# Splitting a real Fourier transform over the model dimension a second time by parity: four matrices of half the rows and half the columns in place of two

## Chip, core and metric

One core of one Trainium2 chip runs the kernel. The metric is the device time of one execution in microseconds (us); lower is better. Three runs of the kernel before took 1491.76, 1490.05 and 1491.19 us, median 1491.19 us.

## What is computed

```python
x = A_x                                    # (1, 2048, 576), float32
xn = _layernorm(x, axis=-1)
X = jnp.fft.rfft2(xn, axes=(-2, -1))       # over the 2048 rows (s) and the 576 columns (d)
X = X * (w_r + 1j * w_i)                   # weights (2048, 289)
y = jnp.fft.irfft2(X, s=(2048, 576), axes=(-2, -1))
g = x @ w_gate; u = x @ w_up               # (576, 4608) each
return x + y + (_sigmoid(g) * u) @ w_down  # w_down (4608, 576)
```

## The kernel before

Two computations share the core: a gated MLP, and a spectral filter (a two-dimensional real Fourier transform, a product with complex weights, and the inverse).

**The MLP sets the pace.** The 2048 rows are worked in two passes of 1024, and each pass runs 36 units, one for each 128 of the 4608 hidden columns (`unit`, L522). A unit has seven products of seven 512-column matmuls each (L541, tiles pA, pB, pE in PSUM). After every second unit, eight `down` steps (L586) of twelve 288-column matmuls (L597, tile po) add to the output accumulators on VectorE (L602).

**The filter is interleaved.** Between a unit's products stands a call of `beside`, which moves each active generator on by one step, up to its next `yield`. All work of the filter lies in the second pass. Its three stages begin at fixed steps (`U1, U2, U3`, L37), so that one of their tiles starts every 4.5 to 4.8 steps. Below they are called stages U1, U2 and U3:

- U1, `phase1b` (L335, 16 tiles of 128 rows): normalise a tile (L345), fold it about column 288 into an even and an odd half of 289 columns (`eo`, L348), transpose it on TensorE (tile pf, L357), and multiply by two 289x290 matrices, cosine and sine (tile pd, L372). Then the first part of the transform over the rows (tile pa, L383).
- U2, `phase2` (L388, 16 tiles): the second part over the rows (pb, L411), the product with the complex weights on VectorE (z and t2, L418 to L420), and the first part of the inverse (pc, L427).
- U3, `phase3` (L432, 16 tiles): the rest of the inverse over the rows (py, L453), transpose (pz, L465), the inverse over d with two 289x290 matrices (pe, L482), and VectorE adds of the result onto the accumulators (L486 to L489).

**Precision.** The matmuls take operands of type fp32r. `split` (L175) makes of a value a high part (a ScalarE copy into an fp32r tile, L176) and a low part (a VectorE subtraction, L177). A product is the sum of high x high, low x high and high x low. The 289 rows of a transform are two blocks of 128 and a remainder of 33. The remainder's high part, low part and high part again are stacked into one operand of 99 rows (`rp`, fr and z3r), so that one matmul does for it. A transform has thus 2 x (2 x 3 + 1) = 14 matmuls of 290 columns. The stationary operand of each is a 128-column tile of the transposed data (fh, fl, fr in U1; z3h, z3l, z3r in U3), the moving one a row block of the constant matrix (cf, or dit).

**What sets the order.** The tile framework schedules each engine's instructions when the program is built, with waits between engines; on the chip each engine then takes its own in that order. The PSUM tiles pf, pd, pa, pb, pc, py, pz, pe and po all come from one pool of two buffers (`pair`, L141). Most tiles of a stage have one buffer.

In the tables of the page, PE is TensorE, PEld its loading of stationary operands, DVE is VectorE, ACT is ScalarE, POOL is GpSimd, and SPq the queue that issues DMAs.

Of the kernel before, what the change touches and what calls it, by code (L numbers as in the profile page):

```python
# [24 lines left out]
FR = HD + 1 - 2 * P  # L25
# [14 lines left out]
KOF = np.array(list(range(1, 257)) + [0] + list(range(257, 289)))  # L40
# [19 lines left out]
def _constants():  # L60
    out = {}

    d = np.arange(HD + 1)[:, None]
    ang = 2 * np.pi * ((d * KOF[None, :]) % D) / D
    t = np.zeros((P, 2, 5, NQ), np.float32)
    for e, v in ((0, np.cos(ang)), (1, -np.sin(ang))):
        m = np.zeros((HD + 1, NQ))
        m[:, :KD] = v
        if e == 0:
            m[HD] *= 0.5  # L70
        else:
            m[0] = m[HD] = 0.0
            m[:, 256] = m[:, 288] = 0.0
        hi, lo = _split(m)
        for part, w in ((0, hi), (1, lo)):
            t[:, e, 2 * part] = w[:P]
            t[:, e, 2 * part + 1] = w[P:2 * P]
        t[:3 * FR, e, 4] = np.concatenate([hi[2 * P:], hi[2 * P:], lo[2 * P:]])
    out["cf"] = t.reshape(P, 10 * NQ)
# [27 lines left out]
    dd = np.arange(HD + 1)
    ang = 2 * np.pi * ((KOF[:, None] * dd[None, :]) % D) / D
    a = np.where((KOF == 0) | (KOF == HD), 1.0, 2.0)[:, None] / (D * S)
    co = np.zeros((KD, NQ))  # L110
    si = np.zeros((KD, NQ))
    co[:, :HD + 1] = a * np.cos(ang)
    si[:, 1:HD] = (a * np.sin(ang))[:, 1:HD]
    si[256] = 0.0
    si[288] = 0.0
    t = np.zeros((P, 2, 5, NQ), np.float32)
    for e, m in ((0, co), (1, si)):
        hi, lo = _split(m)
        for part, w in ((0, hi), (1, lo)):
            t[:, e, 2 * part] = w[:P]  # L120
            t[:, e, 2 * part + 1] = w[P:2 * P]
        t[:3 * FR, e, 4] = np.concatenate([hi[2 * P:], hi[2 * P:], lo[2 * P:]])
    out["di"] = t.reshape(P, 10 * NQ)
    out["id"] = np.eye(P, dtype=np.float32)
    return out
# [3 lines left out]
def spectral_glu_kernel(ctx: ExitStack, tc: tile.TileContext, x, w_r, w_i, w_gate, w_up, w_down, out):  # L129
# [45 lines left out]
    def split(hi, lo, src, eng=None):  # L175
        nc.scalar.activation(hi, src, AF.Copy)  # L176
        (eng or nc.vector).tensor_tensor(lo, src, f32(hi), op=OP.subtract)  # L177
# [157 lines left out]
    def phase1b(t):  # L335
# [16 lines left out]
        nc.scalar.activation(rp[:, :, 2, :], rem, AF.Copy)  # L352
        yield
        pt = pair(f"pf{t}")
        for e in range(2):
            for k in range(2):
                nc.tensor.transpose(pt[:, 0, (2 * e + k) * P:(2 * e + k + 1) * P], eo[:, e, k * P:(k + 1) * P], idf)  # L357
            nc.tensor.transpose(pt[:3 * FR, 1, e * P:(e + 1) * P].bitcast(F32R), rp[:, e].rearrange("p a b -> p (a b)"), idr)
# [4 lines left out]
        nc.scalar.activation(fr[:3 * FR], pt[:3 * FR, 1, :2 * P].rearrange("p (e s) -> p e s", e=2), AF.Copy)  # L363
        yield
        pd = pair(f"pd{t}")
        for e in range(2):
            steps = []
            for k in range(2):
                steps += [(fh[:, e, k, :], cf[:, e, k, :]), (fl[:, e, k, :], cf[:, e, k, :]), (fh[:, e, k, :], cf[:, e, 2 + k, :])]
            steps.append((fr[:3 * FR, e, :], cf[:3 * FR, e, 4, :]))  # L370
            for n, (l, r) in enumerate(steps):
                nc.tensor.matmul(pd[:, e, :NQ], l, r, start=n == 0, stop=n == len(steps) - 1)  # L372
# [15 lines left out]
    def phase2(i):  # L388
# [25 lines left out]
        nc.scalar.activation(sw[N1:], pb[:N1, :, :KD], AF.Copy)
        z = pool.tile([P, 2, KD], F32, tag="z", name=f"z{i}")
        t2 = pool.tile([P, 2, KD], F32, tag="t2", name=f"t2{i}")
        for q, k in ((slice(0, 256), slice(1, 257)), (slice(256, 257), slice(0, 1)), (slice(257, KD), slice(257, KD))):
            nc.vector.tensor_tensor(z[:, :, q], wr[:, :, k], pb[:, :, q], op=OP.mult)  # L418
# [13 lines left out]
    def phase3(t):  # L432
# [33 lines left out]
        v = pz[:3 * FR, 1, :256].rearrange("p (c a s) -> p c a s", c=2, a=2)
        for sl in range(2):
            nc.tensor.transpose(v[:, :, sl, :].bitcast(F32R), rp[:, sl].rearrange("p a b -> p (a b)"), idr)
# [4 lines left out]
        nc.scalar.activation(zr[:3 * FR], pz[:3 * FR, 1, :256].rearrange("p (c s) -> p c s", c=2), AF.Copy)  # L473
# [2 lines left out]
        for e in range(2):
            steps = []
            for k in range(2):
                steps += [(zh[:, k, e, :], di[:, e, k, :]), (zl[:, k, e, :], di[:, e, k, :]), (zh[:, k, e, :], di[:, e, 2 + k, :])]
            steps.append((zr[:3 * FR, e, :], di[:3 * FR, e, 4, :]))  # L480
            for n, (l, r) in enumerate(steps):
                nc.tensor.matmul(pe[:, e, :NQ], l, r, start=n == 0, stop=n == len(steps) - 1)  # L482
        od = pool.tile([P, HD + 1], F32, tag="od", name=f"od{t}")
        nc.scalar.activation(od, pe[:, 1, :HD + 1], AF.Copy)
# [9 lines left out]
    def stage1():  # L494
        pool = room("1")
        R["cf"] = cf = pool.tile([P, 2, 5, NQ], F32R, name="cf")
        load_r(cf, con["cf"].rearrange("p (e k n) -> p e k n", e=2, k=5))
        yield

    def stage2():  # L500
        pool = room("2")
# [2 lines left out]
        zh = pool.tile([P, 2, NQ], F32R, name="zh")
        zl = pool.tile([P, 2, NQ], F32R, name="zl")
        for z in (zh, zl):
            nc.vector.memset(f32(z)[:, :, KD:], 0.0)
        R["zz"] = [(zh, zl)]
# [247 lines left out]
```

## Time and profile before

| | |
|---|---|
| median of three runs | 1491.19 us (1490.05 to 1491.76) |
| the profiled execution | 1492.63 us, of which 1490.8 us span |
| mean granted TensorE clock | 0.993 |
| PE busy, PEld busy | 1449.1 us (97%), 1277.1 us (86%) |
| DVE, ACT, POOL busy | 963.6 us (65%), 579.5 us (39%), 23.0 us (2%) |
| matmuls of L541 (MLP, first step), L597 (second step) | 3577, 3456 |
| matmuls of pd (L372), of pe (L482) | 224, 224 |

The span runs from the first instruction to the last. A row of the timeline gives the start in us, the time in us, the engine, the line, the operation with output and inputs, the shape, and how many instructions are merged in the row; in brackets stands how long the engine was idle before it and what released it. A matmul's time in such a row is from its issue to the modelled end of its pipeline, and neighbours overlap in it. How fast they follow on each other is read from the starts. A row of the windows gives, for one stretch of the span, each engine's busy time with the count of instructions, then the granted clock, the DMA share and GB/s.

### The profile page before, as it was taken

The page shows a single profiled execution, that of the slowest core. Times are in us where ns is not written, and L with a number is a line of the kernel's source. Part 1 is how long each engine was busy: PE and PEld are TensorE (multiplying, and loading weights), DVE is VectorE, ACT ScalarE, POOL GpSimd, SP SyncE. Part 2 cuts the span into 40 slices and gives each one's busy share as a digit, 9 for nine tenths or more (in the row PEclk, how much of TensorE's full clock was granted, in tenths as well). Part 3 has the DMA queues.
Part 4 walks back from the last instruction along what each step waited for, and adds up shares of the span by engine and source line. Part 5 has one row for each costly group of instructions (what it writes and reads, how often), then busy time and mean ns, then how long its engine had stood idle before and what let it go on. Part 6 is the DMA issues. An engine that isn't in the chain of part 4 may idle for free.

```text
span 1490.8 us, 21461 instructions
## 1 busy us (share of the span) xinstructions
PE 1449.1 (97%) x8229; PEld 1277.1 (86%) x8229; DVE 963.6 (65%) x1628; ACT 579.5 (39%) x965; POOL 23.0 (2%) x44
## 2 busy tenths in 40 slices
PE   3899999999999999999999999999999999999998
PEld 3688888888888888887888888888888899898897
DVE  7989977777777777777465555455566554554543
ACT  3534444333344443334343434343444333333321
POOL 1100000000000000011000000000000000000000
PEclk9899999999999999999999999999999999999999
DMA  6388666666665666665964645487777566753522
GB/s 200 136 280 269 233 219 229 242 239 229 229 216 213 222 231 239 226 212 215 287 215 157 199 160 195 153 258 226 226 251 233 213 234 201 232 166 136 186 94 64
DMA packets 152630, 311.79 MB, mean 209 GB/s; under 512 B 14160, under 2 KB 79952, under 8 KB 147664
## 3 DMA queue, kind: packets, MB, share of 16 engines
q1 hardware_dynamic: 152528, 310.42, 61.7%
q8 instruction: 65, 1.06, 0.3%
q14 instruction: 37, 0.30, 0.1%
HBM read 189.98 MB, written 120.39 MB: 208 GB/s over the span
## 4 chain that ended last, share of the span: by engine, by line
PE 90%; DVE 4%; SPq 2%; ACT 1%; DMA 1%; issue 1%; DVEq 0%; ACTq 0%
PE po L597 29%; PE pB L541 22%; PE pE L541 14%; PE pA L541 14%; PE pd L372 2%; PE pe L482 2%; PE px L322 1%; PE pa L383 1%; PE pc L427 1%; PE pb L411 1%; SPq L257 1%; PE py L453 1%; DMA xt<-in_A_x 0%; DVE xs L284 0%; PE pf L357 0%
## 5 line engine op out<-in xcount | busy, mean ns | idle before, releaser
L597 PE MATMUL po<-wd,hh 128*128 128x288 f32 x2304 | 402.4, 296 | 2.3 <-ACT hh L582 1.7
L541 PE MATMUL pB<-X,w 128*128 128x512 f32 (+1 forms) x1533 | 391.8, 390 | 2.4 <-ACT v L555 1.3
L602 DVE TENSOR_TENSOR acc<-acc,po 128x576 f32<-128x576 f32 x288 | 216.2, 753 | 235.3 <-PE po L597 231.7
L597 PEld LDWEIGHTS po<-wd,hh 128*128 128x128 f32 x2304 | 344.6, 189 | 16.2 <-DVE acc L602 2.5
L541 PEld LDWEIGHTS pB<-X,w 128*128 128x128 f32 x1533 | 278.3, 188 | 55.9 <-ACT v L555 2.7
L541 PE MATMUL pA<-X,w 128*128 128x512 f32 (+1 forms) x1022 | 264.2, 392 | 1.6 <-ACT X L325 0.9
L541 PE MATMUL pE<-X,w 128*128 128x512 f32 (+1 forms) x1022 | 263.5, 393 | 0.7 <-ACT X L325 0.7
L597 PE MATMUL po<-wd,hl 128*128 128x288 f32 x1152 | 246.9, 295 | 0.0
L541 PEld LDWEIGHTS pA<-X,w 128*128 128x128 f32 x1022 | 189.6, 190 | 38.0 <-ACT X L325 1.4
L541 PEld LDWEIGHTS pE<-X,w 128*128 128x128 f32 x1022 | 187.0, 191 | 34.4 <-ACT X L325 1.0
L597 PEld LDWEIGHTS po<-wd,hl 128*128 128x128 f32 x1152 | 186.7, 189 | 0.2 <-DVE hl L583 0.2
L565 ACT ACTIVATE g<-pB 128x512 f32<-128x512 f32 (+1 forms) x73 | 43.3, 593 | 217.2 <-PE pB L541 216.8
L583 DVE TENSOR_TENSOR hl<-y,hh 128x1024 fp32r<-128x1024 f32 x72 | 87.9, 1222 | 25.1 <-ACT hh L582 25.1
L204 ACT ACTIVATE w<-raw 128x1152 fp32r<-128x1152 f32 x36 | 42.1, 1168 | 137.0 <-PE pE L541 115.3
L580 DVE TENSOR_TENSOR y<-y,g 128x1024 f32<-128x1024 f32 x72 | 88.2, 1224 | 5.6
L582 ACT ACTIVATE hh<-y 128x1024 fp32r<-128x1024 f32 x72 | 75.5, 1048 | 10.9 <-DVE y L580 10.5
L569 DVE TENSOR_TENSOR y<-v,pE 128x512 f32<-128x512 f32 (+1 forms) x73 | 49.6, 679 | 45.1 <-PE pE L541 44.9
L562 DVE TENSOR_TENSOR y<-v,pE 128x512 f32<-128x512 f32 (+1 forms) x73 | 49.4, 676 | 38.4 <-ACT v L561 38.1
L548 ACT ACTIVATE pB<-pA 128x512 f32<-128x512 f32 (+1 forms) x73 | 41.9, 574 | 74.0 <-PE pA L541 74.0
L561 ACT ACTIVATE v<-pB 128x512 f32<-128x512 f32 (+1 forms) x73 | 43.2, 592 | 51.0 <-PE pB L541 50.7
L558 ACT ACTIVATE g<-pA 128x512 f32<-128x512 f32 (+1 forms) x73 | 43.1, 591 | 49.3 <-PE pA L541 49.3
L204 ACT ACTIVATE w<-tt 128x768 fp32r<-128x768 f32 x72 | 59.7, 829 | 1.9 <-DVE tt L220 1.9
(123 smaller groups left out, 1303.8 us busy)
## 6 DMA issues: line engine op xcount, KB each, us to landing
wsp<-w SPq DMA_DIRECT2D x36, 2240.0 KB
w<-wsp SPq DMA_DIRECT2D x252, 320.0 KB
wdsp<-wd SPq DMA_DIRECT2D x36, 576.0 KB
wd<-wdsp SPq DMA_DIRECT2D x36, 576.0 KB
std<-in_B_w_down SPq DMA_DIRECT2D x36, 288.0 KB
raw<-in_B_w_gate SPq DMA_DIRECT2D x72, 128.0 KB
raw<-in_B_w_up SPq DMA_DIRECT2D x72, 128.0 KB
sc<-x SPq DMA_DIRECT2D x16, 290.0 KB
```

The lines of the kernel that those rows point to most:

```text
L204: nc.scalar.activation(o[:, :, :3, :], src, AF.Copy)
L541: nc.tensor.matmul(bank[b], w[:, WB[kb], sw, :], X[:, XA[ka], sx, cols], start=b not in seen and j == 0, stop=j == len(STEPS) - 1, skip_gr ...
L558: nc.scalar.activation(g[:, 0], bank["A"], AF.Sigmoid)
L561: nc.scalar.activation(v[:, 1], bank["B"], AF.Copy)
L562: nc.vector.tensor_tensor(y[:, 1], v[:, 1], bank["E"], op=OP.add)
L565: nc.scalar.activation(g[:, 1], bank["B"], AF.Sigmoid)
L569: add = lambda: nc.vector.tensor_tensor(y[:, 0], v[:, 0], bank["E"], op=OP.add)
L580: nc.vector.tensor_tensor(Y, Y, G_, op=OP.mult)
L582: ends.extend([first, lambda: nc.scalar.activation(hh, Y, AF.Copy), lambda: nc.vector.tensor_tensor(hl, Y, f32(hh), op=OP.subtract)])
L583: lambda: nc.vector.tensor_tensor(hl, Y, f32(hh), op=OP.subtract)])
L597: nc.tensor.matmul(pd[:, b, :HD], l[:, c, cols], w[:, k, b * HD:(b + 1) * HD], start=g == 0 and l is hh and k == 0, stop=g == G - 1 and l ...
L602: nc.vector.tensor_tensor(a, a, pd[:, :, :HD], op=OP.add)
```

## The change

The folded halves of U1 are folded once more, about column 144: the even part of the cosine half goes with the even frequencies, its odd part with the odd ones, and the other way round for the sine half. Each of the four combinations is a transform with 145 rows (one block of 128 and a remainder of 17) and 146 or 144 columns. The spectrum's columns are stored in the order of the even frequencies, a zero column, then the odd ones (KOF). The remainders of both parities are stacked into one operand of 6 x 17 = 102 rows, used with two matrices that have zeros in the other parity's rows. The inverse in U3 is split in the same way, and its four results are joined again on VectorE.

In numbers, for each tile: pd and pe are 4 x 4 = 16 matmuls of 146 or 144 columns (14 of 290 before); the transposes stay six. In U1 VectorE has two more operations (f4) and one more small subtraction, ScalarE two more small copies (four of 34 columns in place of two of 66) and a copy of one column. In U2 the product with the weights is done in two column groups in place of three, and reads every second column of the weights. In U3 VectorE has four more operations (cs, 145 or 144 columns), and its four adds onto the accumulators read cs. The constants cf and dit have 12 x 146 = 1752 columns in place of 2900.

```diff
+QD = D // 4 + 1
+HQ = NQ // 2
+QR = QD - 128
-FR = HD + 1 - 2 * P
-KOF = np.array(list(range(1, 257)) + [0] + list(range(257, 289)))
+KOF = np.array(list(range(0, KD, 2)) + [-1] + list(range(1, KD, 2)))
...
-        rp = pool.tile([P, 2, 3, FR], F32R, tag="rp", name=f"rp{t}")
-        rem = eo[:, :, 2 * P:2 * P + FR]
-        split(rp[:, :, 0, :], rp[:, :, 1, :], rem)
-        nc.scalar.activation(rp[:, :, 2, :], rem, AF.Copy)
+        nc.scalar.activation(eo[:, 0, HD:HD + 1], xb[:, HD:HD + 1], AF.Copy)
+        f4 = pool.tile([P, 2, 2, HQ + 1], F32, tag="f4", name=f"f4{t}")
+        for i, op in ((0, OP.add), (1, OP.subtract)):
+            nc.vector.tensor_tensor(f4[:, i, :, :QD], eo[:, :, :QD], eo[:, :, QD - 1:HD + 1][:, :, ::-1], op=op)
+        rp = pool.tile([P, 2, 3, 2, QR], F32R, tag="rp", name=f"rp{t}")
+        for c, rem in ((0, f4[:, :, 0, P:QD]), (1, f4[:, ::-1, 1, P:QD])):
+            split(rp[:, c, 0], rp[:, c, 1], rem)
+            nc.scalar.activation(rp[:, c, 2], rem, AF.Copy)
...
-        for e in range(2):
-            steps = []
-            for k in range(2):
-                steps += [(fh[:, e, k, :], cf[:, e, k, :]), (fl[:, e, k, :], cf[:, e, k, :]), (fh[:, e, k, :], cf[:, e, 2 + k, :])]
-            steps.append((fr[:3 * FR, e, :], cf[:3 * FR, e, 4, :]))
-            for n, (l, r) in enumerate(steps):
-                nc.tensor.matmul(pd[:, e, :NQ], l, r, start=n == 0, stop=n == len(steps) - 1)
+        for c in range(2):
+            for par, q in ((0, slice(0, HQ + 1)), (1, slice(HQ + 1, NQ))):
+                n = q.stop - q.start
+                w = cf[:, c, par, :, :n]
+                steps = ((fh[:, c, par], w[:, 0]), (fl[:, c, par], w[:, 0]), (fh[:, c, par], w[:, 1]), (fr[:6 * QR, c], w[:6 * QR, 2]))
+                for i, (l, r) in enumerate(steps):
+                    nc.tensor.matmul(pd[:, c, q], l, r, start=i == 0, stop=i == len(steps) - 1)
...
-        for q, k in ((slice(0, 256), slice(1, 257)), (slice(256, 257), slice(0, 1)), (slice(257, KD), slice(257, KD))):
+        for q, k in ((slice(0, HQ), slice(0, KD, 2)), (slice(HQ + 1, NQ), slice(1, KD, 2))):
             nc.vector.tensor_tensor(z[:, :, q], wr[:, :, k], pb[:, :, q], op=OP.mult)
             nc.vector.tensor_tensor(t2[:, :, q], wi[:, :, k], sw[:, :, q], op=OP.mult)
...
+        for b in range(2):
+            for c in range(2):
+                par = b ^ c
+                w = di[:, c, par]
+                steps = ((zh[:, par, c], w[:, 0]), (zl[:, par, c], w[:, 0]), (zh[:, par, c], w[:, 1]), (zr[:6 * QR, c], w[:6 * QR, 2]))
+                for i, (l, r) in enumerate(steps):
+                    nc.tensor.matmul(pe[:, b, c * (HQ + 1):(c + 1) * (HQ + 1)], l, r, start=i == 0, stop=i == len(steps) - 1)
...
-        nc.vector.tensor_tensor(lo, lo, od, op=OP.subtract)
-        nc.vector.tensor_tensor(lo, lo, pe[:, 0, :HD + 1], op=OP.add)
+        for c, lo_op, up_op in ((0, OP.add, OP.subtract), (1, OP.subtract, OP.add)):
+            nc.vector.tensor_tensor(cs[:, c, :QD], p0[:, c, :QD], od[:, c, :QD], op=lo_op)
+            nc.vector.tensor_tensor(cs[:, c, QD:][:, ::-1], p0[:, c, :QD - 1], od[:, c, :QD - 1], op=up_op)
+        co, si = cs[:, 0], cs[:, 1]
+        nc.vector.tensor_tensor(lo, lo, co, op=OP.add)
+        nc.vector.tensor_tensor(lo, lo, si, op=OP.subtract)
```

The change moves instructions on every engine. On TensorE, this is the 15th tile of U1 before, from the last transpose into pf to the first products of pd; pE is a product of the MLP, fh, fl and fr are the high part, the low part and the remainder of the transposed tile:

```order
L358 MATMUL pf_8654<-idr,rp_8613 99x128
L541 MATMUL pE_0_8474<-X,w_8273 128x512 x7
L372 MATMUL pd_8681<-cf,fh_8661 128x290
L372 MATMUL pd_8681<-cf,fl_8662 128x290
L372 MATMUL pd_8681<-cf,fh_8661 128x290 x2
L372 MATMUL pd_8681<-cf,fl_8662 128x290
L372 MATMUL pd_8681<-cf,fh_8661 128x290
L372 MATMUL pd_8681<-cf,fr_8663 128x290
```

And the same place now (f is the twice folded tile):

```order
L369 MATMUL pf_8787<-idr,rp_8743 102x128
L557 MATMUL pE_0_8598<-X,w_8381 128x512 x7
L383 MATMUL pd_8814<-cf,fh_8794 128x146
L383 MATMUL pd_8814<-cf,fl_8795 128x146
L383 MATMUL pd_8814<-cf,fh_8794 128x146
L383 MATMUL pd_8814<-cf,fr_8796 128x146
L383 MATMUL pd_8814<-cf,fh_8794 128x144
```

The first product with the remainder fr stood five places behind the first one with fl; it stands two places behind it.

ScalarE at the same tile before, from the copy that makes fh to the copy that makes fr (rp is the remainder of the next tile):

```order
L176 ACTIVATE fh_8661<-pf_8654 128x512
L176 ACTIVATE rp_8752<-eo_8749 128x2x33
L352 ACTIVATE rp_8752<-eo_8749 128x2x33
L363 ACTIVATE fr_8663<-pf_8654 99x256
L176 ACTIVATE ah_8696<-pd_8681 64x290
```

And now:

```order
L182 ACTIVATE fh_8794<-pf_8787 128x512
L182 ACTIVATE rp_8891<-f_8888 128x34
L363 ACTIVATE rp_8891<-f_8888 128x34
L182 ACTIVATE rp_8891<-f_8888 128x34
L363 ACTIVATE rp_8891<-f_8888 128x34
L374 ACTIVATE fr_8796<-pf_8787 102x256
```

Two more copies of the next tile's remainder stand ahead of fr.

TensorE at the second tile of U3 before, from the first product of pe:

```order
L482 MATMUL pe_11462<-dit,z3h_11427 128x290
L541 MATMUL pE_0_11446<-X,w_11230 128x512 x4
L482 MATMUL pe_11462<-dit,z3l_11428 128x290
L482 MATMUL pe_11462<-dit,z3h_11427 128x290 x2
L482 MATMUL pe_11462<-dit,z3l_11428 128x290
L482 MATMUL pe_11462<-dit,z3h_11427 128x290
L541 MATMUL pE_0_11446<-X,w_11230 128x512
L482 MATMUL pe_11462<-dit,z3r_11429 128x290
```

And now:

```order
L493 MATMUL pe_11551<-dit,z3h_11516 128x146
L557 MATMUL pE_0_11535<-X,w_11312 128x512 x3
L493 MATMUL pe_11551<-dit,z3l_11517 128x146
L493 MATMUL pe_11551<-dit,z3h_11516 128x146
L557 MATMUL pE_0_11535<-X,w_11312 128x512 x2
L493 MATMUL pe_11551<-dit,z3r_11518 128x146
```

Between z3l and z3r stood four products of pe and one of the MLP; there stand one of pe and two of the MLP.

More of the change, by code (lines that the diff above doesn't have):

```diff
@@ L61, in _constants, with pack @@
     out = {}
[L63 to L73, printed above, removed]
-        hi, lo = _split(m)
[L75 to L79, printed above, removed]
+    d = np.arange(QD)[:, None]
+    ks = (np.append(KOF[:HQ], -1), KOF[HQ + 1:])
+    def pack(main, rem, par, m):
+        hi, lo = _split(m)
+        main[:, 0], main[:, 1] = hi[:P], lo[:P]
+        for i, w in enumerate((hi, hi, lo)):
+            rem[(2 * i + par) * QR:(2 * i + par + 1) * QR] = w[P:]
+    t = np.zeros((P, 2, 2, 3, HQ + 1), np.float32)
+    for c, fun in enumerate((np.cos, lambda a: -np.sin(a))):
+        for par, k in enumerate(ks):
+            m = np.where(k < 0, 0.0, fun(2 * np.pi * ((d * k) % D) / D))
+            m[QD - 1] *= 0.5
+            if c:
+                m[0] = 0.0
+                m[:, (k == 0) | (k == HD)] = 0.0
+            n = len(k)
+            pack(t[:, c, par, :2, :n], t[:, c, par, 2, :n], par, m)
+    out["cf"] = t.reshape(P, 12 * (HQ + 1))
     s1 = np.arange(N1)
@@ L104, in _constants @@
     out["bm"] = b.reshape(P, 4 * P)
[L107 to L123, printed above, removed]
+    dd = np.arange(QD)
+    t = np.zeros((P, 2, 2, 3, HQ + 1), np.float32)
+    for c, fun in enumerate((np.cos, np.sin)):
+        for par in range(2):
+            k = KOF[par * HQ:(par + 1) * HQ, None]
+            a = np.where(k < 0, 0.0, np.where((k == 0) | (k == HD), 1.0, 2.0)) / (D * S)
+            m = np.zeros((HQ, HQ + 1))
+            m[:, :QD] = a * fun(2 * np.pi * ((k * dd) % D) / D)
+            if c:
+                m[:, 0] = 0.0
+                m[(k[:, 0] == 0) | (k[:, 0] == HD)] = 0.0
+                if not par:
+                    m = -m
+            pack(t[:, c, par, :2], t[:, c, par, 2], par, m)
+    out["di"] = t.reshape(P, 12 * (HQ + 1))
     out["id"] = np.eye(P, dtype=np.float32)
@@ L472, in phase3 @@
         split(zh, zl, pz[:, 0, :].rearrange("p (a c s) -> p a c s", a=2, c=2))
-        nc.scalar.activation(zr[:3 * FR], pz[:3 * FR, 1, :256].rearrange("p (c s) -> p c s", c=2), AF.Copy)
+        nc.scalar.activation(zr[:6 * QR], pz[:6 * QR, 1, :256].rearrange("p (c s) -> p c s", c=2), AF.Copy)
         yield
         pe = pair(f"pe{t}")
[L476 to L482, printed above, removed]
@@ L483, in phase3 @@
-        od = pool.tile([P, HD + 1], F32, tag="od", name=f"od{t}")
-        nc.scalar.activation(od, pe[:, 1, :HD + 1], AF.Copy)
+        for b in range(2):
+            for c in range(2):
+                par = b ^ c
[3 more added lines that the diff above has]
+                    nc.tensor.matmul(pe[:, b, c * (HQ + 1):(c + 1) * (HQ + 1)], l, r, start=i == 0, stop=i == len(steps) - 1)
@@ new lines, in phase3 @@
+        p0, p1 = (pe[:, b, :2 * (HQ + 1)].rearrange("p (c q) -> p c q", c=2) for b in range(2))
+        od = pool.tile([P, 2, HQ + 1], F32, tag="od", name=f"od{t}")
+        nc.scalar.activation(od, p1, AF.Copy)
+        cs = pool.tile([P, 2, HD + 1], F32, tag="cs", name=f"cs{t}")
+        for c, lo_op, up_op in ((0, OP.add, OP.subtract), (1, OP.subtract, OP.add)):
+            nc.vector.tensor_tensor(cs[:, c, :QD], p0[:, c, :QD], od[:, c, :QD], op=lo_op)
+            nc.vector.tensor_tensor(cs[:, c, QD:][:, ::-1], p0[:, c, :QD - 1], od[:, c, :QD - 1], op=up_op)
@@ L490, in phase3 @@
+        nc.vector.tensor_tensor(up, up, si[:, 1:HD], op=OP.add)
         if t < TPP:
@@ L503, in stage2 @@
         load_r(bm, con["bm"].rearrange("p (k m) -> p k m", k=4))
[L504 to L508, printed above, removed]
+        R["zz"] = [pool.tile([P, 2, NQ], dt, name=n) for n, dt in (("z", F32), ("t2", F32), ("zh", F32R), ("zl", F32R))]
+        for z in R["zz"][:2]:
+            nc.vector.memset(z[:, :, HQ:HQ + 1], 0.0)
         yield
```

51 lines of the change are left out of this document (24 added, 27 removed).

## The prediction

> **What bounds the kernel now.** I read the page first: the busy shares, then the chain that ended last.
>
> ```profile
> span 1490.8 us, 21461 instructions
> PE 1449.1 (97%) x8229; PEld 1277.1 (86%) x8229; DVE 963.6 (65%) x1628; ACT 579.5 (39%) x965; POOL 23.0 (2%) x44
> ...
> PE 90%; DVE 4%; SPq 2%; ACT 1%; DMA 1%; issue 1%; DVEq 0%; ACTq 0%
> ```
>
> TensorE is busy for 97% of the span and makes 90% of the chain. The change touches three stages only, so I asked for the windows that hold U1, U2 and U3.
>
> ```profile
> 722.00:965.00 243.00, 241.86 (x1412) 209.69 (x1412) 132.38 (x226) 95.99 (x204) 1.62 (x13) 1.00 0.58 189
> 965.00:1195.00 230.00, 229.82 (x1296) 201.41 (x1294) 134.92 (x235) 97.15 (x150) 0.00 (x0) 1.00 0.74 237
> 1195.00:1460.00 265.00, 264.90 (x1570) 236.81 (x1569) 131.42 (x207) 90.18 (x183) 0.00 (x0) 1.00 0.52 172
> ```
>
> In each of them TensorE has work in flight for all but 0.1 to 1.2 us, at full granted clock, while VectorE is busy for 50 to 59% and ScalarE for 34 to 42%. So what counts is how many ns TensorE's queue gains or loses at each instruction of the change; work added on VectorE or ScalarE is free unless TensorE waits for it. This is the 15th tile of U1 in the timeline:
>
> ```profile
> 934.98 0.30 PE L358 MATMUL pf<-idr,rp 128*99 128x128 f32 x1
> 935.12 1.83 PE L541 MATMUL pE<-X,w 128*128 128x512 f32 x7
> 935.38 0.60 ACT L176 ACTIVATE fh<-pf 128x512 fp32r<-128x512 f32 x1 [3.21 <-PE pf L358]
> 935.43 0.83 DVE L348 TENSOR_TENSOR eo<-xb 128x289 f32<-128x289 f32 x2
> 936.17 0.69 DVE L177 TENSOR_TENSOR fl<-pf,fh 128x512 fp32r<-128x512 f32 x1
> 936.35 0.26 ACT L176 ACTIVATE rp<-eo 128x66 fp32r<-128x66 f32 x1 [0.37 <-DVE eo L348]
> 936.51 0.24 ACT L352 ACTIVATE rp<-eo 128x66 fp32r<-128x66 f32 x1
> 936.79 0.29 PE L372 MATMUL pd<-cf,fh 128*128 128x290 f32 x1
> 936.89 0.38 ACT L363 ACTIVATE fr<-pf 99x256 fp32r<-99x256 f32 x1
> 936.91 0.19 PEld L372 LDWEIGHTS pd<-cf,fl 128*128 128x128 f32 x1 [0.16 <-DVE fl L177]
> ...
> 937.56 0.19 PEld L372 LDWEIGHTS pd<-cf,fr 99*128 99x128 f32 x1
> 937.69 0.29 PE L372 MATMUL pd<-cf,fr 99*128 99x290 f32 x1
> ...
> 938.78 0.40 PE L541 MATMUL pA<-X,w 128*128 128x512 f32 x1
> ```
>
> Seven products of the MLP cover the time in which ScalarE and VectorE make fh and fl. The load of fl waits 0.16 us, then all runs through. The remainder fr is ready at 937.27, and its load starts at 937.56: 0.29 us to spare.
>
> **The change part by part.**
>
> *TensorE's products.* Wide pairs (load and matmul) are counted from start to start. The first U3 tile that I read shows them without a wait:
>
> ```profile
> 1291.53 0.39 ACT L473 ACTIVATE z3r<-pz 99x256 fp32r<-99x256 f32 x1 [0.76 <-DVE z3l L177]
> 1291.58 0.29 PE L482 MATMUL pe<-dit,z3h 128*128 128x290 f32 x1
> 1291.71 0.30 PE L482 MATMUL pe<-dit,z3l 128*128 128x290 f32 x1
> ...
> 1293.46 1.79 PE L541 MATMUL pA<-X,w 128*128 128x512 f32 x7
> ```
>
> 14 pairs take 1293.46 - 1291.58 = 1.88 us, 134 ns each. In U1 they take 938.78 - 936.79 = 1.99, of which some 0.10 is fl's load that nothing hid, so 1.89. Now there are 16 pairs of 146 or 144 columns. No pair of that width is in the trace; the nearest rows are pairs of 128 and of 256 columns:
>
> ```profile
> 37.59 0.82 PE L322 MATMUL px<-idf,xs 128*128 128x128 f32 x6
> 36.22 0.52 PE L541 MATMUL pA<-X,w 128*128 128x256 f32 x3
> ...
> 934.95 0.17 PEld L358 LDWEIGHTS pf<-idr,rp 128*99 128x99 f32 x1
> 935.06 1.46 PEld L541 LDWEIGHTS pE<-X,w 128*128 128x128 f32 x7
> ...
> 1289.69 0.39 PE L468 MATMUL pz<-idr,rp 128*99 128x128 f32 x2
> 1289.92 1.83 PE L541 MATMUL pE<-X,w 128*128 128x512 f32 x7
> ```
>
> Six transposes of 128 columns span 0.82 us with one tail of 0.27: (0.82 - 0.27) / 5 = 0.11 us apart. Three matmuls of 256 columns: (0.52 - 0.28) / 2 = 0.12 apart, though twice as wide. Loads follow on each other 0.11 apart (934.95 to 935.06), and the two fp32r transposes take 1289.92 - 1289.69 = 0.23 together. So a short pair is set by its load of 128 columns, not by what streams through. I take 0.111: 16 x 0.111 = 1.78 us, 0.11 less than 14 wide pairs. Over 32 transforms that gains 3.5 us, though the multiplications are halved. Bounds: at 0.12 each the transform is 1.92 us (a loss of 1.1 us in all); at 0.095, if part of the next load hides behind the stream, 1.52 (a gain of 11.7 us).
>
> The Trainium skill, page "TensorE: Matmul & The Clock Gate", section "Back-to-back issue gap", gives about 81 ns for a pair of load and matmul at 128 columns. By that, an estimate, 16 pairs would be about 1.3 us, and the gain about 19 us. The same page's section "LDWEIGHTS (loading the stationary operand)" gives P / 1.2 ns for P columns, 107 ns at 128, and speaks against the change. The rows side with the second.
>
> *The remainder comes earlier in the order.* Its copy on ScalarE starts 0.03 us after the low part is done, in U1 (936.86 to 936.89) as in U3 (released by z3l), and takes 0.38 us. Before, four or more wide pairs hid that. Now one short pair lies between. In the tile above, fl's load starts at 936.91, the next at 937.02, and fr's would start at 937.13; fr is ready at 937.27, with some 0.03 to the load: 0.17 us late. ScalarE also has four remainder copies ahead of fr in place of two, 0.16 apart, the last started at 936.83, so fr starts near 936.99 and is 0.27 late. In U3 the low part doesn't hold TensorE up, the load would start at 1291.80 and z3r is ready at 1291.92: 0.15 late. What the load waits, all of TensorE waits.
>
> Where ScalarE does another operation before the remainder, the scheduler had left filling between z3l and z3r, and now leaves less:
>
> ```profile
> 1227.21 1.05 ACT L582 ACTIVATE hh<-y 128x1024 fp32r<-128x1024 f32 x1
> 1228.16 0.38 ACT L473 ACTIVATE z3r<-pz 99x256 fp32r<-99x256 f32 x1
> 1228.22 0.40 PE L541 MATMUL pE<-X,w 128*128 128x512 f32 x1
> 1228.59 0.40 PE L482 MATMUL pe<-dit,z3r 99*128 99x290 f32 x1
> ```
>
> Here z3r lands at 1228.54, and TensorE already waits a little for it. That moment is set by hh and stays. Ahead of z3r stood six wide pairs of this transform, so that eight were left (8 x 0.134 = 1.07 us); now three short ones stand there, with the same five MLP products, and 13 are left (13 x 0.111 = 1.44 us). The transform ends 0.37 us later where the shorter pairs alone would end it 0.11 sooner: the wait takes 0.48.
>
> Counting over the 32 transforms in the orders of TensorE and ScalarE: 8 have whole accumulation steps between transpose and transform and lose nothing; 16 lose as in the plain cases (nine in U1 at about 0.22, seven in U3 at 0.15: 3.0 us); 8 have another ScalarE operation in the way (three in U1, five in U3, taken at 0.46 each: 3.7 us). Sum 6.7 us. The bounds are 0, if the remainder's copy turns out earlier, and 10, if each of the 24 lost 0.4.
>
> *VectorE and ScalarE.*
>
> ```profile
> L348 DVE TENSOR_TENSOR eo<-xb 128x289 f32<-128x289 f32 x32 | 13.5, 456 | 6.0 <-PE pf L358 5.6
> L352 ACT ACTIVATE rp<-eo 128x66 fp32r<-128x66 f32 x16 | 4.0, 249 | 0.0
> L418 DVE TENSOR_TENSOR z<-wr,pb 128x512 f32<-128x512 f32 x16 | 11.0, 690 | 22.4 <-ACT sw L414 15.8 <-DMA w<-wsp 3.3 <-PE pB L541 3.1
> L418 DVE TENSOR_TENSOR z<-wr,pb 128x64 f32<-128x64 f32 x16 | 3.4, 215 | 0.0
> L418 DVE TENSOR_TENSOR z<-wr,pb 128x2 f32<-128x2 f32 x16 | 2.4, 151 | 0.0
> ```
>
> U1: two f4 operations of 290 columns cost what eo does, 2 x 0.456, and one small subtraction up to 0.25: VectorE goes from 132 to about 151 of 243 us; ScalarE gets some 0.75 a tile, 12 us. The f4 of the next tile stands where eo stood, between fh and fl, so fl keeps its time. U3: four cs of 145 columns, between 0.215 (64) and 0.456 (289), say 0.30 each: 1.2 a tile, 19 us in 265 at 50% busy. The next U3 tile comes a dozen us later, and pe is read out sooner than before (four short operations in place of four long), so I cost this at nothing. If that cover were gone, up to 1.2 us a tile would show. U2: six products (2 x (0.690 + 0.215 + 0.151) = 2.11 us) become four of 0.456 (1.82), and the first product of pc stands up to one MLP matmul (0.23) earlier in the order in most tiles: between 16 x 0.29 = 4.6 us gained and 16 x 0.23 = 3.7 us waited, taken as 0, for the two follow from each other. That a column step of two in the weights costs nothing is assumed; no row has one. If it doubled the stream, each product would be some 0.30 longer.
>
> The Trainium skill, page "SBUF — State Buffer", section on partitions and ports, says that two fp32 hits in a 16-byte line keep full speed, which a step of two still gives; no run here shows it.
>
> *DMA.* cf and dit shrink from 1450 KB to 897 KB and are loaded once each, a step ahead; nothing waits for them.
>
> **The sum.** -3.5 + 6.7 = +3.2 us. The profiled execution took 1492.63 us with a span of 1490.8, 1.4 above the median; on the median the forecast is 1491.2 + 3.2 = 1494.4 us. A measurement of this kernel tells about 0.2% (3.0 us) from no change, so this lies on the line between the same and slower.
>
> **Rivals.**
>
> - *Not slower: the remainder hides.* Place: the fourth pair. The copy to fr needs the transposes alone; its wait for the low part is inferred from semaphores. If in the new program it starts when ScalarE is free, it is done more than 0.15 us sooner, which is where it decides for the 16 plain cases. Then -3.5 + 3.7 = +0.2: 1491.4 us. Against: the wait is there in both tiles above.
> - *Faster: short pairs run below the load's pace*, at 0.095. -11.7 + 6.7 = -5.0: 1486.2 us. By the page's 81 ns it would be about 1479. Against: the 0.11 of loads and transposes.
> - *Slower: a short pair costs as much as a wide one* (0.134, were columns streamed at half rate below 256). 16 x 0.134 = 2.14, +0.26 x 32 = +8.2, and the remainder's waits shrink to about 5.5: +13.7, 1504.9 us. Against: the fp32r transposes of 128 columns, 0.23 for two.
> - *Slower: U2's strided products* take 4 x 0.76 = 3.0 in place of 1.82 us, and pc waits 0.9 us in each of 16 tiles: +14 on the forecast, 1508 us.
>
> **How the numbers follow.** The forecast has a chance of 0.55. Its own range is 1491 to 1498, half of it beyond +3.0: slower 0.30, same 0.25. The hidden remainder 0.20 (same 0.15, faster 0.05). Short pairs below the load's pace 0.07, faster. Short as wide 0.10 and strided products 0.08, slower. Together faster 0.12, same 0.40, slower 0.48. The range 1488.5 to 1501 holds the forecast's case, the hidden remainder and the near parts of the others.
>
> **What the new profile would show.** Starts within a run of pd or pe 0.11 us apart (0.13: short as wide; under 0.10: below the load). Loads of fr and z3r idle for 0.1 to 0.5 us, released by ScalarE's copies, in about 24 transforms. The first product of pc waiting longer for z in U2 would speak for the strided products. I would be wrong if no load of fr waits, or if TensorE waits in U3 for accumulators or banks that the cs operations hold.

## The result, and the profile after

The changed kernel takes 1511.78 us (median of 4 runs, 1510.09 to 1512.78) against 1491.47 of the kernel before beside it: ratio 1.0137, 95% interval 1.0119 to 1.0154. It is slower by 20.3 us. The forecast was 1494.4 us with a range that ended at 1501: slower had been called the likeliest outcome, and the size was missed by 17 us.

The page of the profiled execution of the changed kernel (1512.78 us), first its busy shares and then the chain that ended last, by engine:

```profile
span 1511.0 us, 21741 instructions
...
PE 1452.4 (96%) x8293; PEld 1276.6 (84%) x8293; DVE 986.9 (65%) x1708; ACT 584.2 (39%) x1013; POOL 22.6 (1%) x44
...
PE 84%; DVE 7%; DMA 4%; ACT 2%; issue 1%; SPq 1%; POOL 0%; DVEq 0%; POOLq 0%; ACTq 0%
```

TensorE's busy time grew by 3.3 us, about what two stretches at half clock add (shown below), and the span by 20.2. TensorE's share of the chain fell from 90 to 84%, VectorE's rose from 4 to 7 and that of transfers from 1 to 4. So the time went into waits. The windows of U1, U2 and U3, at the same times as before, tell which stage:

```profile
722.00:965.00 243.00, 227.67 (x1337) 195.68 (x1336) 136.38 (x257) 93.74 (x237) 1.30 (x13) 0.99 0.56 181
965.00:1195.00 230.00, 229.98 (x1305) 201.55 (x1304) 132.09 (x205) 97.93 (x154) 0.00 (x0) 1.00 0.71 226
1195.00:1460.00 265.00, 263.51 (x1584) 233.46 (x1583) 143.55 (x265) 89.89 (x181) 0.00 (x0) 1.00 0.57 188
```

In U1 TensorE is busy for 227.67 us, where it was 241.86 before, and gets through 1337 matmuls in place of 1412. It is idle for 15.3 of the 243 us, where it was for 1.1. U2 is as full as it was, U3 lacks 1.4 us. The waits of U1 name the place. First the kernel before (the columns are us in total, times, longest):

```profile
PEld pa L383 <- ACT ah L176: 6.6, 20, 0.5
...
DVE xb L284 <- DMA xb<-in_A_x: 5.6, 8, 1.2
...
PEld pa L383 <- DVE al L177: 0.6, 2, 0.3
```

Then the changed kernel:

```profile
DVE xb L290 <- DMA xb<-in_A_x: 22.3, 11, 4.0
...
PEld pa L394 <- ACT ah L182: 15.1, 19, 2.9
...
PE pa L394 <- ACT ah L182: 8.8, 6, 2.5
...
PEld pa L394 <- DVE al L183: 3.9, 4, 2.0
...
PE pa L394 <- DVE al L183: 2.4, 2, 1.6
```

TensorE's loads for pa, the step behind the changed transform, wait 19.0 us for the split of its result (ah on ScalarE, al on VectorE) in place of 7.2. Not all of that stops the matmuls: by the rows of PE they stand still at pa for 11.2 us, which is most of the 15.3. The kernel before has no such row. VectorE waits 22.3 us in its normalisation (the line of xb) for the transfer of xb, in place of 5.6.

**One tile, before.** ScalarE and VectorE make ah and al in turns, four times a tile. In the timeline of the kernel before, the normalisation of a later tile follows when the last al is done:

```profile
831.24 0.45 DVE L177 TENSOR_TENSOR al<-pd,ah 64x290 fp32r<-64x290 f32 x1 [0.47 <-ACT ah L176]
...
832.48 0.46 DVE L177 TENSOR_TENSOR al<-pd,ah 64x290 fp32r<-64x290 f32 x1 [0.78 <-ACT ah L176]
...
833.41 0.46 DVE L177 TENSOR_TENSOR al<-pd,ah 64x290 fp32r<-64x290 f32 x1 [0.47 <-ACT ah L176]
...
834.32 0.58 DVE L284 TENSOR_SCALAR xb<-xb,mv,rstd 128x576 f32<-128x576 f32 x1 [0.45 <-DMA xb<-in_A_x]
```

**The same tile, after:**

```profile
843.29 0.41 ACT L182 ACTIVATE ah<-pd 64x290 fp32r<-64x290 f32 x1
...
843.43 1.31 PE L557 MATMUL pB<-X,w 128*128 128x512 f32 x5
...
845.68 0.58 DVE L290 TENSOR_SCALAR xb<-xb,mv,rstd 128x576 f32<-128x576 f32 x1 [2.80 <-DMA xb<-in_A_x]
...
846.29 0.46 DVE L183 TENSOR_TENSOR al<-pd,ah 64x290 fp32r<-64x290 f32 x1
...
846.79 0.41 ACT L182 ACTIVATE ah<-pd 64x290 fp32r<-64x290 f32 x1 [3.09 <-DVE al L183]
...
847.25 0.61 PE L394 MATMUL pa<-ah,am 128*128 128x290 f32 x1 [2.51 <-ACT ah L182]
```

The third ah is ready at 843.70. But in VectorE's order the normalisation now stands between the second and the third al, and it waits 2.80 us for its transfer. VectorE takes its instructions in order, so al waits too, the fourth ah waits for al, and TensorE stands still for 2.51 us. Then it pays once more:

```profile
844.00:847.20 3.20, 0.74 (x4) 0.28 (x2) 1.04 (x2) 0.41 (x1) 0.00 (x0) 1.00 0.12 30
847.20:850.60 3.40, 3.35 (x12) 3.16 (x13) 1.15 (x2) 1.25 (x2) 0.00 (x0) 0.50 0.10 22
```

Behind the pause the granted clock is 0.50 for 3.4 us (the last column but two), which is another 1.7 us lost.

The same happens around 792 us, and there the pause is not at pa:

```profile
791.79 0.58 DVE L290 TENSOR_SCALAR xb<-xb,mv,rstd 128x576 f32<-128x576 f32 x1 [3.95 <-DMA xb<-in_A_x]
...
793.84 1.43 PE L557 MATMUL pB<-X,w 128*128 128x512 f32 x5 [1.55 <-ACT v L577]
...
797.00:800.00 3.00, 3.00 (x16) 3.00 (x15) 0.76 (x1) 0.00 (x0) 0.00 (x0) 0.59 0.00 0
```

The normalisation holds up al, al holds up the next ah, and behind ah in ScalarE's order stands v, which a product of the MLP waits for. After this pause and one of 0.57 us the clock is 0.50 from 796.0 to 799.4, another 1.7 us.

**A second place.** In tile 0 of U1, ScalarE's order has changed. Before, the first ah went ahead of hh, the high part of the MLP's result:

```profile
726.42 0.41 ACT L176 ACTIVATE ah<-pd 64x290 fp32r<-64x290 f32 x1 [1.83 <-PE pd L372]
...
726.73 1.05 ACT L582 ACTIVATE hh<-y 128x1024 fp32r<-128x1024 f32 x1
...
726.87 0.45 DVE L177 TENSOR_TENSOR al<-pd,ah 64x290 fp32r<-64x290 f32 x1 [0.39 <-ACT ah L176]
```

After, hh and on VectorE hl (its low part) go first, and pa waits:

```profile
727.76 1.06 ACT L598 ACTIVATE hh<-y 128x1024 fp32r<-128x1024 f32 x1 [1.90 <-DVE y L596]
...
728.73 0.39 ACT L182 ACTIVATE ah<-pd 64x290 fp32r<-64x290 f32 x1
...
728.86 1.23 DVE L599 TENSOR_TENSOR hl<-y,hh 128x1024 fp32r<-128x1024 f32 x1 [1.13 <-ACT hh L598]
...
730.00 0.45 DVE L183 TENSOR_TENSOR al<-pd,ah 64x290 fp32r<-64x290 f32 x1
...
730.93 0.40 PE L394 MATMUL pa<-ah,am 128*128 128x290 f32 x1 [1.68 <-ACT ah L182]
```

The same happens in tiles 11 and 14. In eight tiles, the example above among them, the normalisation now stands directly ahead of the low parts or between them; before, that was so in one.

**What came as forecast.** The short pairs and the remainder in one tile of the changed U1:

```profile
907.65 0.39 ACT L374 ACTIVATE fr<-pf 102x256 fp32r<-102x256 f32 x1
...
907.85 0.27 PE L383 MATMUL pd<-cf,fh 128*128 128x146 f32 x1
...
908.09 0.34 PE L383 MATMUL pd<-cf,fr 102*128 102x146 f32 x1
...
908.71 0.28 PE L383 MATMUL pd<-cf,fh 128*128 128x146 f32 x1
...
909.61 1.36 PE L557 MATMUL pA<-X,w 128*128 128x512 f32 x5
```

The last eight pairs take 909.61 - 908.71 = 0.90 us, 0.112 each. The first product of fr starts 0.24 us after the one before it, 0.13 late: ScalarE's copy ends at 908.04.

### The profile page after: what moved, and what is told of

Read it like the earlier page. It is cut to its first block, busy times and chain, and to the rows that moved or that the text cites. A ratio compares the mean times of both kernels' runs of the same rounds, so it can differ in the third digit from the quotient of the medians.

```text
span 1511.0 us, 21741 instructions
## 1 busy us (share of the span) xinstructions
PE 1452.4 (96%) x8293; PEld 1276.6 (84%) x8293; DVE 986.9 (65%) x1708; ACT 584.2 (39%) x1013; POOL 22.6 (1%) x44
## 4 chain that ended last, share of the span: by engine, by line
PE 84%; DVE 7%; DMA 4%; ACT 2%; issue 1%; SPq 1%; POOL 0%; DVEq 0%; POOLq 0%; ACTq 0%
PE po L613 29%; PE pB L557 20%; PE pE L557 13%; PE pA L557 13%; DMA xb<-in_A_x 2%; PE pe L493 2%; PE px L328 1%; PE pc L436 1%; PE pa L394 1%; PE pd L383 1%; PE pb L422 1%; PE py L462 1%; DVE y L596 1%; ACT hh L598 1%; SPq L263 1%
```

## The theories

- **A, the order.** On ScalarE and VectorE the new program has another order around ah and al. The normalisation, which waits for a transfer, and hh and hl stand ahead of them, and TensorE waits at pa.
- **B, the buffer.** The new copy of one column of xb on ScalarE (L355) is a second reader of xb. It keeps xb's buffer, so that the next transfer starts late and the normalisation waits.
- **C, on record.** The remainder's waits are what costs, only larger than they were costed.
- **D, why the order changed.** Either the new fold f4, one buffer more ahead of the transposes, pulls the fold forward, or the framework that orders the instructions at build time plans products of under 256 columns much longer than they are, and so ah and al too late.

## The experiments

All times are medians. The kernel before, run beside them, took 1491.56 to 1491.71 us.

### Which stage

**fwd_only**: U1 as changed, with U3's old inverse in the new column order.

```diff
-                steps = ((zh[:, par, c], w[:, 0]), (zl[:, par, c], w[:, 0]), (zh[:, par, c], w[:, 1]), (zr[:6 * QR, c], w[:6 * QR, 2]))
...
+                steps += [(zh[:, k, e, :], di[:, e, k, :]), (zl[:, k, e, :], di[:, e, k, :]), (zh[:, k, e, :], di[:, e, 2 + k, :])]
+            steps.append((zr[:3 * FR, e, :], di[:3 * FR, e, 4, :]))
```

> Keeps the split in U1 and the new column order; U3 has its old inverse again (14 wide products, four adds and no cs). Theory A, the order: with the split of U1, VectorE's normalisation of a later tile (which waits for the transfer of xb) stands between the low parts al, and hh and hl stand ahead of the first ah and al, so that TensorE waits for ah and al at pa. Then all of the loss is in U1: 1508 to 1514 us, with U1's waits as in the changed kernel. Theory B, the buffer: the one-column copy of xb on ScalarE holds xb's buffer, so that transfers come late: the same time, for that copy is still there. Theory C, on record: the remainder's waits are larger than they were costed, in U1 and U3 alike; then half of the 20 us goes, 1499 to 1503.

Measured: 1508.23 us (1503.77 to 1510.38), ratio 1.0110 (1.0091 to 1.0129). Most of the loss, some 16 of 20 us, lies in U1. C falls short, A and B hold.

**inv_only**: U3 as changed, with U1's old fold and products in the new column order.

```diff
-                steps = ((fh[:, c, par], w[:, 0]), (fl[:, c, par], w[:, 0]), (fh[:, c, par], w[:, 1]), (fr[:6 * QR, c], w[:6 * QR, 2]))
...
+                steps += [(fh[:, e, k, :], cf[:, e, k, :]), (fl[:, e, k, :], cf[:, e, k, :]), (fh[:, e, k, :], cf[:, e, 2 + k, :])]
+            steps.append((fr[:3 * FR, e, :], cf[:3 * FR, e, 4, :]))
```

> Keeps the split in U3 and the new column order; U1 has its old fold and its 14 wide products again. Theories A and B: nothing of the 20 us is left, 1490 to 1494 us, by the record's terms for U3 alone (a gain of 1.8 in short pairs, a loss of 3.4 in waits for the remainder). Theory C: 1499 to 1503.

Measured: 1492.80 us (1492.21 to 1494.24), ratio 1.0009 (1.0000 to 1.0018). U3 costs 1.2 us, where the record's terms for it alone give 1.6. In U3 the sum came out.

### Buffer or fold

**eo_dve**: the one column is halved on VectorE; ScalarE no longer reads xb.

```diff
-        nc.scalar.activation(eo[:, 0, HD:HD + 1], xb[:, HD:HD + 1], AF.Copy)
+        nc.vector.tensor_scalar(eo[:, 0, HD:HD + 1], eo[:, 0, HD:HD + 1], 0.5, None, op0=OP.mult)
```

> The changed kernel, with the one-column copy of xb on ScalarE replaced by a halving of that column on VectorE, which reads no xb. Theory B: xb comes free with the fold, the loss goes: 1492 to 1497 us. Theory A: the order on VectorE is nearly the same, so the time is too: 1508 to 1514. Theory C: 1509 to 1513.

Measured: 1508.31 us (1505.42 to 1514.28), ratio 1.0119 (1.0094 to 1.0145). B falls: the copy is not what costs.

**before_stage**: the kernel before, with a buffer f4 between fold and transposes and two VectorE operations that fill it.

```diff
+        f4 = pool.tile([P, 2, HD + 2], F32, tag="f4", name=f"f4{t}")
+        for e in range(2):
+            nc.vector.tensor_tensor(f4[:, e, :HD + 1], eo[:, e, :HD + 1], eo[:, e, :HD + 1], op=OP.max)
...
-        rem = eo[:, :, 2 * P:2 * P + FR]
+        rem = f4[:, :, 2 * P:2 * P + FR]
...
```

> The kernel before, with one buffer more between the fold and the transposes: two VectorE operations of 289 columns copy eo into f4, and remainder and transposes read f4. Products, ScalarE's work and column order are those of before. Theory A: an earlier fold moves the loads and normalisations against the low parts; part of the loss comes back without any split, 1494 to 1502 us, with VectorE waiting for xb over 10 us in U1. hh still stands behind the first ah, so that part of the loss stays away. Theories B and C: 1490 to 1493, no change.

Measured: 1492.07 us (1490.87 to 1493.76), ratio 1.0008 (0.9998 to 1.0017). Its waits in U1:

```profile
DVE xb L284 <- DMA xb<-in_A_x: 7.2, 8, 1.6
...
PEld pa L386 <- ACT ah L176: 5.4, 17, 0.5
```

Theory A as I first had it, with the deeper fold as its cause, missed here: the extra stage, with two more VectorE operations a tile, costs nothing that can be told. What is left to upset the order is the short products, and with them the two more copies of the remainder. The first is the second half of D.

### The order alone

These kernels keep the whole change and only force VectorE's or ScalarE's order, by edges that set the order of issue and add no wait for data: `behind(a, b)` puts a behind b on their engine.

**norm_late**: in six places the normalisation is put behind the last al.

```diff
-        norm(xb[:, :D], xb[:, :D], t)
+        nx = norm(xb[:, :D], xb[:, :D], t)
+        if t >= 4:
+            behind(nx, LAST_AL[t - 4])
...
```

> The changed kernel with VectorE's order changed in six places of U1 only: the normalisation of tile t stands behind the last low part of tile t-4. Theory A: the waits of al for VectorE go (in the trace 1.7 and 0.7 us around 792, 1.8 at 815, 0.8 at 831, 2.7 and 0.6 at 844, and the half clock behind them, some 2 us): 1501 to 1504 us. If the normalisation is no cause: 1509 to 1513.

**hh_late**: in three places hh is put behind the first ah, and hl behind the first al.

```diff
+            i = nc.scalar.activation(hh, Y, AF.Copy)
+            if "ah0" in R:
+                behind(i, R.pop("ah0"))
...
```

> The changed kernel with three places of order put back: in U1's tiles 0, 11 and 14 hh stands behind the first ah on ScalarE, and hl behind the first al on VectorE, as before; nothing else moves. Theory A: TensorE's waits of 1.85, 1.88 and 1.63 us at pa there go: 1506 to 1508 us. If hh first is no cause: 1509 to 1513.

**both_late**: both edits.

> Both edits of order together, the split and its products untouched. Theory A: the two add, 1495 to 1499 us; what stays over before is the remainder's waits and the clock. If the times do not add: over 1501.

| | us | ratio to before, interval | against the changed kernel |
|---|---|---|---|
| norm_late | 1499.59 | 1.0057 (1.0042 to 1.0072) | -12.2 |
| hh_late | 1508.16 | 1.0114 (1.0097 to 1.0131) | -3.6 |
| both_late | 1496.59 | 1.0035 (1.0022 to 1.0048) | -15.2 |

The waits of norm_late in U1:

```profile
PEld pa L404 <- ACT ah L182: 11.7, 19, 2.1
...
DVE xb L296 <- DMA xb<-in_A_x: 10.5, 7, 2.5
```

And those of both_late:

```profile
DVE xb L296 <- DMA xb<-in_A_x: 10.9, 8, 3.2
...
PEld pa L404 <- ACT ah L182: 6.6, 18, 1.2
...
PEld pa L404 <- DVE al L183: 4.0, 4, 1.8
```

Nine places of order, with all of the new work left in, are worth 15 of the 20 us, and the two edits add (12.2 + 3.6 = 15.8). Norm_late gained more than was expected; hh_late ended just past its range, for in it pa waits longer for al (5.8 us where the changed kernel has 3.9). Its gain alone is about what a measurement can tell; both_late, 3.0 us under norm_late, has it again. In both_late the loads of pa still wait 10.6 us, 3.4 more than before, mostly at places that I left as they were.

The idle time of TensorE in U1 goes with it: 15.3 us in the changed kernel, 11.9 in hh_late, 8.0 in norm_late, 5.0 in both_late and 1.1 before. Above before, norm_late has 6.9 us of it and both_late 3.9; with U3's 1.2 that makes 8.1 and 5.1, where the times are 8.0 and 5.0 us above before. In the changed kernel 14.2 us more idle time, 3.4 us for the two stretches at half clock and U3's 1.2 make 18.8 of the 20.3.

### Wait or place

**xb3**: a third buffer for xb, meant to let the transfers start earlier.

```diff
-        xb = pool.tile([P, D + 2], F32, tag="xb", name=f"xb{t}", bufs=2)
+        xb = pool.tile([P, D + 2], F32, tag="xb", name=f"xb{t}", bufs=3)
```

> The changed kernel with three buffers for xb in place of two; the order on VectorE stays as it is, with the normalisation ahead of or between the low parts, and the transfers start a tile earlier. If it is the wait for the transfer that costs (theory A): VectorE's wait for xb falls under 6 us in U1 and the time to 1499 to 1503 us. If the normalisation's place alone costs (0.58 us of work each): 1506 to 1510. If neither: 1509 to 1513.

Measured: 1512.37 us (1509.32 to 1513.72), ratio 1.0136 (1.0121 to 1.0150), and VectorE still waits 17.5 us for xb. This did not test what it was meant to. The build used the third buffer to normalise one tile further ahead, again right behind that tile's transfer, so that the pattern stayed and only the tile's number changed.

**xb3_pin**: three buffers, and the normalisation held at its place ahead of the low parts, behind the fold of tile t-2.

```diff
+        if t >= 2:
+            behind(nx, EO[t - 2])
...
```

> The changed kernel with three buffers for xb, and the normalisation of tile t held behind the fold (eo) of tile t-2 on VectorE. So it stands ahead of the low parts in nine places, two more than in the changed kernel, but its transfer starts a tile earlier, when eo of tile t-3 is done. If the wait for the transfer costs (theory A): VectorE's wait for xb under 5 us in U1, and 1498 to 1503 us, near norm_late's 1499.6. If the place costs, whatever has landed: 1508 to 1514.

Measured: 1498.43 us (1497.33 to 1499.89), ratio 1.0047 (1.0030 to 1.0064). Its waits in U1:

```profile
PEld pa L402 <- ACT ah L182: 11.6, 19, 2.1
...
DVE xb L296 <- DMA xb<-in_A_x: 1.2, 2, 0.8
```

The normalisation stands ahead of the low parts as often as in the changed kernel or more (in two tiles ahead of all four, no longer between them), but its tile has landed, and 13 us are gone. So it is the wait for the transfer, with the low parts queued behind it, and not VectorE's 0.58 us of work.

### Why the order changed

**wide256** and **wide200**: U1's products stream 256, or 200, columns in place of 146 or 144. The surplus goes to columns of PSUM that nothing reads.

```diff
+WQ = 256
...
-            for par, q in ((0, slice(0, HQ + 1)), (1, slice(HQ + 1, NQ))):
+            for par in range(2):
+                q = slice(par * WQ, (par + 1) * WQ)
...
```

> The changed kernel with U1's 16 products widened from 146 or 144 to 256 moving columns each: they stream on into the next rows of cf, the surplus columns of PSUM are not read, and ah and al read the 145 wanted columns of each parity. The work on TensorE grows. Theory D, the planned length: the schedule is made with a length for a product under 256 columns that is far above the 0.111 us of the trace, so that ah and al were planned late and the normalisation, hh and hl were put ahead of them. At 256 columns the schedule comes out close to before's (ah ahead of hh, al ahead of the normalisation at most places). Then TensorE gives some 16 x 16 x 0.015 = 4 us for the wider stream and wins back 12 to 15: 1498 to 1503 us. If the order is not what costs the time, more streaming can only cost: 1512 to 1517.

> As the kernel with 256 columns, with 200 columns in each of U1's products: fewer columns than there, more than in the changed kernel. The schedule comes out like the changed kernel's (hh ahead of the first ah, the normalisation ahead of al). Theory D, the planned length of a product under 256 columns: the order decides, so 1506 to 1512 us, some 15 us slower than with 256 columns. If the 256-column kernel won by something on the chip itself that grows with the columns, this one lies between: 1498 to 1505.

VectorE's order in one tile of U1 as the build makes it, in the changed kernel (xb is the normalisation):

```
998 L183 TENSOR_TENSOR rp_7343<-f_7340,rp_7343 128x34 x2
999 L354 TENSOR_TENSOR eo_7465<-xb_7423 128x289 x2
1000 L290 TENSOR_SCALAR xb_7716<-xb_7716,mv,rstd 128x576
1001 L183 TENSOR_TENSOR al_7241<-pd_7223,ah_7240 64x290 x2
```

and with 256 columns, where the normalisation comes behind the low parts:

```
1001 L355 TENSOR_TENSOR eo_7466<-xb_7424 128x289 x2
1002 L184 TENSOR_TENSOR al_7242<-pd_7224,ah_7241 64x290 x2
...
1006 L184 TENSOR_TENSOR al_7242<-pd_7224,ah_7241 64x290
1007 L291 TENSOR_SCALAR xb_7717<-xb_7717,mv,rstd 128x576
```

Measured: 256 columns 1493.55 us (1492.59 to 1495.31), ratio 1.0015 (1.0005 to 1.0024); 200 columns 1530.09 us (1528.81 to 1532.77), ratio 1.0260 (1.0245 to 1.0274). The waits of U1 with 256 columns:

```profile
PEld pa L396 <- ACT ah L183: 6.6, 19, 0.6
...
DVE xb L291 <- DMA xb<-in_A_x: 4.8, 5, 1.4
```

and with 200:

```profile
DVE xb L291 <- DMA xb<-in_A_x: 37.5, 12, 7.4
...
PEld pa L396 <- ACT ah L183: 24.0, 17, 5.9
```

With 75% more columns streamed, the kernel is 18 us faster than the changed kernel, and with 200 columns 18 us slower. The products' own time can't do that: from start to start the pairs take 0.112, 0.112 and 0.120 us for 146, 200 and 256 columns (the median of each kernel's pd). What changes is the order. Both went further than expected: at 256 columns pa's loads wait little more than before (7.4 us, with 0.8 for al) and TensorE idles in U1 for 1.0 us, and at 200 the normalisation stands ahead of or between the low parts in ten tiles and waits up to 7.4 us. So the width of the products brings the order about: the remainder's two more copies are in all three. That the build plans the products of 146 and 200 columns too long, and the wider of them longer, is inferred from these orders; the plan's own lengths were not tried out, nor any width between 200 and 256.

### Versions with the remainder last

**inv_rem**: inv_only, with U3's four remainder products behind the twelve others. **wide_rem**: wide256 with the same edit.

```diff
+        for last in range(2):
...
+                        if (i == 3) == last:
...
```

> The split in U3 alone (U1 with its old fold and products), and in U3 the four products of the remainder stand behind the twelve others. The waits for z3r (2.1 us in ten tiles in the kernel with the remainder fourth) go: 1490.0 to 1491.2 us, where that kernel had 1492.8. If the remainder's wait is only moved to another place: 1492 to 1494.

> The split in both stages, U1 with 256 columns a product, and in U3 the remainder's four products last. From 1493.6 us with the 256 columns alone, the 2.1 us of waits for z3r go: 1490.8 to 1492.2 us. That is no better than before: U1's wider pairs cost 0.120 us each, 16 of them 1.92 us against 1.90 for 14 wide ones. If the waits are only moved: 1493 to 1495.

In the waits of U3, inv_only has this row, and inv_rem has none for z3r:

```profile
PEld pe L492 <- ACT z3r L482: 2.6, 5, 0.6
```

Measured: inv_rem 1489.40 us (1487.95 to 1490.55), ratio 0.9984 (0.9975 to 0.9993); wide_rem 1490.26 us (1488.28 to 1491.15), ratio 0.9989 (0.9980 to 0.9998); both a little under what was expected. The waits for z3r went and did not come back elsewhere. Both beat the kernel before, inv_rem by 2.3 us, about what a measurement can tell; it is the fastest version of this study.

## Why the prediction was wrong, by its own steps

- **Short pairs at 0.111 us: right.** 0.112 was measured, 16 in 1.79 us. The row that was chosen, the pace of loads, held against the 0.120 of a wider product; of the two loads that were read for it, the first has 99 columns and not 128, which did no harm.
- **The Trainium skill's 81 ns for such a pair** (page "TensorE: Matmul & The Clock Gate", section "Back-to-back issue gap"): the trace disagrees with it, as 0.112 says; the 107 ns that its section "LDWEIGHTS (loading the stationary operand)" gives for the load alone is the nearer. But it does not speak against the change, as the prediction has it: 16 x 0.107 = 1.71 us, an estimate, is less than the 1.88 of 14 wide pairs.
- **The remainder, 6.7 us: mechanism right, size smaller in U1.** From starts, ten products of fr begin over 15 ns late behind another product of pd, 1.6 us together, and ten of z3r in pe, 2.1 us; one more in pd and two in pe that follow a product of the MLP bring this to some 2.2 and 2.8 us. The record had 3.4 for each stage. For U3 the edit tells more: from inv_only to inv_rem the ratio falls by 0.0025, 3.7 us, and from wide256 to wide_rem by 0.0026, each give or take 2 us. For U1 no run took the remainder alone away.
- **U1's added work "cost at nothing": the step that failed.** It was right about the work. These are the added groups and those they were costed by, in the changed kernel:

```profile
L354 DVE TENSOR_TENSOR eo<-xb 128x289 f32<-128x289 f32 x32 | 13.7, 456 | 0.6
...
L359 DVE TENSOR_TENSOR f<-eo 128x290 f32<-128x290 f32 x32 | 13.6, 456 | 2.9 <-PE pf L368 1.6 <-ACT eo L355 1.2
...
L500 DVE TENSOR_TENSOR cs<-pe,od 128x145 f32<-128x145 f32 x32 | 9.7, 304 | 28.0 <-ACT od L496 28.0
...
L429 DVE TENSOR_TENSOR t<-wi,sw 128x290 f32<-128x290 f32 x16 | 7.3, 455 | 0.0
```

  f4 takes 0.456 us and cs 0.304, as costed, and before_stage shows that such an extra stage is free. But the step looked at fh and fl alone ("so fl keeps its time") and took the order of everything else as it stood. It didn't follow the result of the transform to its reader: pd to ah and al, and those to pa. There the new order put a waiting normalisation and hh first. The step had nothing in the sum for this; some 15 us came back when nine places of the order were undone. The rule "free unless TensorE waits for it" was right, and it was not applied to that wait.
- **DMA "nothing waits": right for cf and dit**, for which no wait is listed. The part looked at no other transfer: VectorE now waits 22.3 us in place of 5.6 for that of xb, with low parts behind it. (Of the two sizes the first is in units of 1024 bytes and the second in units of 1000; the profile's list of transfers has 1450 and 876 KB.)
- **U2 at zero: right.** TensorE is busy 229.98 of 230 us, and a product that reads every second column takes 0.455 us, as a contiguous fold of 289 columns does (0.456).
- **The rivals** all went by durations on the chip; none was a wait behind an instruction that had moved ahead. With wide256's order the kernel takes 1493.55 us, within 1 us of the forecast of 1494.4. That bears out the sum only in part, for two differences cancel there: its 16 pairs of 0.120 cost 2.3 us more over U1 than pairs of 0.111, and from the starts its remainder in U1 costs 0.3 us at most, where the record had 3.4.
- **The sign came out by luck.** The loss that was forecast, the remainder's waits less the gain of the short pairs, comes to some 2 us by the runs (2.2 + 3.7 - 3.5). The rest, which wide256 takes back, comes with the order around ah and al, which the prediction did not look at.

## What to carry to other kernels

When instructions are ordered by a build-time schedule, a change of shapes can reorder engines that it doesn't touch: compare the new order on each engine down to the next step that TensorE waits for, above all for instructions that wait on a transfer and now stand ahead of something short and urgent. VectorE, busy for 56% of U1, still cost TensorE some 12 us, by one queued wait in each of half a dozen tiles. To tell a change's work from its order, hold the order by edges of issue, or change the shapes so that the order comes back; a further buffer may only move the pattern by one tile.

## What the runs showed of the hardware

The clock fell after short pauses, though not after each. In the changed kernel TensorE stood still for 2.51 us at 844.74 to 847.25, and the granted clock was 0.50 from 847.2 to 850.6. It was also 0.50 from 796.0 to 799.4, behind pauses of 1.55 and 0.57 us. Behind one of 1.59 us at 815.7 it stayed at 1.00, and so it did in wide200 behind one of 2.77 us at 818.7. So in these traces no single length of a pause tells whether the clock falls. The Trainium skill, page "TensorE: Matmul & The Clock Gate", section "Part 1: The HAM clock gate", puts the fall at an idle window of about 3.4 us or more; here pauses shorter than that were enough, and the half clock lasted about one such window.
